# Weight parts of the first feed-forward interleaved by element, zones lengthened by 64 bytes

## The chip, the cores and the metric

The kernel runs on one core of one Trainium2 chip. The metric is the device time of one execution in microseconds (us); a lower time is better. An execution with a profile records what each engine did: TensorE (PE for matmuls, PEld for the weight loads in front of them), VectorE (DVE), ScalarE (ACT), GpSimd (POOL), and SyncE (SP), which only issues DMAs.

## What is computed

The reference, cut to what matters:

```python
B, H, S, D = 4, 8, 576, 64
# attention: 4 heads see the last 32 keys, 4 heads see every 32nd key
attn = softmax(where(mask, q @ k.T / 8, -1e9)) @ v
x = attn.transpose(0, 2, 1, 3).reshape(2304, 512)
x = ((x @ w_a) * (x @ w_b)) @ w_out                    # first feed-forward, 512 -> 1536 -> 512
y = (sigmoid(x @ w_gate) * (x @ w_val)) @ w_out2        # second feed-forward, same sizes
```

All of it is float32, and the result is held to float32 accuracy. TensorE's fast float32 form keeps fewer bits than float32, so the kernel splits each operand into a high and a low part and adds three products: high by high, low by high, high by low.

## The kernel before

**Memory.** Apart from some small tiles and one tile named `rest`, on-chip memory is cut into zones: twelve weight zones `w0` to `w11` of 12,288 bytes in each partition, four activation zones `x12` to `x15` of 8,192 bytes, and `h16` of 4,096 bytes. In the trace a zone appears as `w0p`, `x12p` and so on. `at(a, n, phase)` gives a view of a zone and makes the zone's tile on first use. In the built program all zones and all slices of them that TensorE reads with the fast float32 form start at distances from each other that are multiples of 512 bytes.

**First feed-forward.** The 2304 tokens are five tiles: four of 512 tokens (4 batches by 128 positions) and one of 256. For each tile the code goes through the 12 blocks `k` of the 1536 inner features. Each block has two products (line 923, from `x12` to `x15`) of 4 chunks by 3 terms, that is 24 matmuls, and, one block later, an output product (line 1013, from `h16`) of 12 matmuls. So a tile is 12 x 36 = 432 matmuls and the five tiles are 2160. Each matmul has its own weight load of 128 columns, which TensorE does while the matmul before it runs. The moving operand is 512 or 256 consecutive floats per partition.

**Its weights.** `convert` makes them during the first tile: 36 slices of 512 floats, three for each `k`. For each slice a DMA brings raw 64-bit words, ACT and DVE build a float32 from each (lines 482 and 491; it stands in every second float of a buffer), ACT writes its high part (line 499) and DVE its low part (line 503). Zone `wk` holds `w_a` high, `w_a` low, `w_b` high, `w_b` low, `w_out` high, `w_out` low, each 512 consecutive floats:

```python
def weight(m, k, h, phase=FIRST):
    return (k * 6 + m * 2 + h) * DM, DM, phase
```

While a tile is in the feed-forward, DVE also does the strided heads of the next tile's attention (lines 781 to 851), whose transposes (line 877) and splits (lines 890 and 894) TensorE and DVE do before that tile starts. PE does small attention matmuls (lines 563, 604 and 618) between its feed-forward matmuls.

**Second feed-forward.** It is done by Strassen's seven products on the same zones, reused in two later phases. All of its 2268 matmuls stand in line 1292, with 384 consecutive floats as moving operand and consecutive floats as weights.

**Order.** A planner at build time works out one list per engine, from estimated costs and due times. Each engine keeps its list; waits are by semaphores. At the start, PE is fed matmuls on a bfloat16 tile of zeros named `nil` (line 423) while it has nothing else to do; their weights are 128 consecutive bfloat16 values, their moving operand 512 columns.

Of the kernel before, what the change touches and what calls it, by code (L numbers as in the profile page):

```python
# [7 lines left out]
F32 = mybir.dt.float32  # L8
F32R = mybir.dt.float32r
# [13 lines left out]
P = 128  # L23
# [54 lines left out]
for _n, (_k, _w) in RINGS.items():  # L78
    if _n not in PLACE:
        PLACE[_n] = TOP  # L80
        TOP += _k * _w


def region_of(a):
    return next((r for r in REGIONS if r[0] <= a < r[0] + r[1]), None)
# [81 lines left out]
class Plan:  # L167
# [16 lines left out]
    def touch(self, op, reads=(), writes=()):  # L184

        for ranges, writing in ((reads, False), (writes, True)):
            for a, n, phase in ranges:
                b = a + n
                r = region_of(a)
                if r and self.phase.get(r, EARLY) != phase:  # L190

                    self.phase[r] = phase
                    c, d = r[0], r[0] + r[1]
                    self.seen = [(c, d, s[2], True) if s[0] < d and c < s[1] else s for s in self.seen]
                kept = []
                for s in self.seen:
                    c, d, other, wrote = s
                    if c < b and a < d and other is not op and (wrote or writing):
                        op.deps.append(other)
                        if writing and a <= c and d <= b:  # L200
                            continue
                    kept.append(s)
                self.seen = kept
                self.seen.append((a, b, op, writing))
        return op

    def add(self, eng, cost, fn, deps=(), key=0.0, take=(), free=(), size=0):
        op = Op()
        op.slack = self.slack
        op.eng, op.cost, op.fn, op.key, op.size = eng, cost, fn, key * 1e3, size  # L210
        op.deps = [d for d in deps if d is not None]
        op.take, op.free, op.slot, op.end = take, free, {}, None
        op.seq = len(self.ops)
        self.ops.append(op)
        for ring, owner in free:
            if ring in PLACE:
                taker, i = owner if isinstance(owner, tuple) else (owner, None)
                rings = [allowed for r, allowed in taker.take if r == ring]
                for allowed in rings if i is None else rings[i:i + 1]:
                    size = RINGS[ring][1]  # L220
                    for s in allowed:
                        a = PLACE[ring] + s * size
                        self.ends.append((a, a + size, op))
        return op
# [88 lines left out]
def dve(n):  # L313
    return (n + 66) / 0.96


def act(n):
    return (n + 105) / 1.2
# [22 lines left out]
def r32(ap):  # L341
    return ap.bitcast(F32)
# [3 lines left out]
def attention_moe_kernel(ctx, tc, qkv, sq, sk, sv, w1, w2, mask, ident, out):  # L346
    nc = tc.nc
    PE, ACT, DVE, POOL = nc.tensor, nc.scalar, nc.vector, nc.gpsimd
    engine = {"ACT": ACT, "DVE": DVE, "POOL": POOL}

    sb = ctx.enter_context(tc.tile_pool(name="sb", bufs=1))
# [10 lines left out]
    tiles = {}  # L362

    def at(a, n, phase=FIRST, dtype=F32):
        r = region_of(a)
        if r is None:
            v = rest[:, a - F0:a - F0 + n]
        else:
            if tiles.get(r, (None,))[0] != phase:
                name = f"{('w', 'x', 'h')[(r[0] >= X0) + (r[0] >= H0)]}{REGIONS.index(r)}"  # L370
                tiles[r] = phase, sb.tile([P, r[1]], F32, tag=name, name=f"{name}p{phase}")
            v = tiles[r][1][:, a - r[0]:a - r[0] + n]
        return v if dtype == F32 else v.bitcast(dtype)

    def xT(i, c):

        return at(X0 + (2 * i + c // 2) * XZONE, XZONE, FIRST, F32R).rearrange("p (c n) -> p c n", c=HK)
# [3 lines left out]
    add, touch = plan.add, plan.touch  # L381

    def buf(op, ring, shape, dtype=F32):
        s = op.slot[ring][0]
        if ring in PLACE:
            return at(PLACE[ring] + s * RINGS[ring][1], shape[1], FIRST, dtype)
        return sb.tile(shape, dtype, tag=f"{ring}{s}", name=f"{ring}{s}")
# [14 lines left out]
    for i, n in enumerate(TILES):  # L402
        begin.append(t)
        k = sum(g.i == i + 1 for g in GROUPS)
# [5 lines left out]
    def weight(m, k, h, phase=FIRST):  # L410

        return (k * 6 + m * 2 + h) * DM, DM, phase
# [37 lines left out]
    def raw(op, dtype=F32):  # L450
        return buf(op, "raw", [P, T * D], dtype)

    def convert(w, need, start=()):
        parts, done, merges = {}, {}, []
        tops = []

        def clear(op):
            for i in op.slot["c"]:
                tops.append(at(PLACE["c"] + i * DM, DM, FIRST, U32))
                POOL.memset(tops[-1], 0)  # L460

        c_top = add("POOL", 1000, clear, start, key=need(0, 0) - AHEAD - 10,
                    take=[("c", F_RING[:1]), ("c", F_RING[1:])])
        for c in range(3 * KF):
            k, m = divmod(c, 3)
            x = {}
            key = need(k, m) - AHEAD
            at_load = key - LEAD

            if k == 0 and m < 2:  # L470
                key -= EARLIER

            def load(op, x=x, k=k, m=m):

                x["raw"] = raw(op, U32)[:, :2 * DM]
                nc.sync.dma_start(
                    out=x["raw"].bitcast(U16)[:, :4 * DM - 1], in_=w[k, m].bitcast(U16)[:, 1:]
                )

            def top(op, x=x):  # L480
                x["t"] = tops[op.slot[f"t{id(w)}"][0]]
                ACT.activation(  # L482
                    out=x["t"].bitcast(F16).rearrange("p (n two) -> p n two", two=2)[:, :, 1],
                    in_=x["raw"].bitcast(BF16).rearrange("p (n four) -> p n four", four=4)[:, :, 2],
                    func=AF.Copy, scale=0.5,
                )

            def merge(op, x=x):
                u = x["raw"].rearrange("p (n two) -> p n two", two=2)[:, :, 0]
                x["f"] = u.bitcast(F32)  # L490
                DVE.scalar_tensor_tensor(  # L491
                    out=u, in0=u, scalar=13, in1=x["t"],
                    op0=ALU.logical_shift_right, op1=ALU.bitwise_or,
                )

            def high_part(op, x=x, k=k, m=m):
                hi, lo = (at(*weight(m, k, i), F32R) for i in range(2))
                parts[m, k] = hi, lo
                ACT.activation(out=hi, in_=x["f"], func=AF.Copy, scale=256.0)

            def low_part(op, x=x, k=k, m=m):
                hi, lo = parts[m, k]
                DVE.scalar_tensor_tensor(
                    out=lo, in0=x["f"], scalar=256.0, in1=r32(hi),
                    op0=ALU.mult, op1=ALU.subtract,
                )

            plan.slack = M2
            a = add("SP", 450, load, start, key=at_load, take=[("raw", (0, 1, 2))], size=1 << 19)
            b = add("ACT", act(512), top, [a, c_top], key, take=[(f"t{id(w)}", (0, 1))])  # L510
            end = c == 3 * KF - 1
            f = add("DVE", dve(512), merge, [b] + merges * end, key,
                    free=[(f"t{id(w)}", b)] + [("c", c_top)] * end)
            merges.append(f)
            g = touch(add("ACT", act(512), high_part, [f], key), (), [weight(m, k, 0)])
            h = touch(add("DVE", dve(512), low_part, [g], key, free=[("raw", a)]), (), [weight(m, k, 1)])
            done[m, k] = g, h
            plan.slack = 0
        return parts, done
# [481 lines left out]
    for n, g in enumerate(GROUPS):  # L1001
        if g.i == 0:
            attention(g, n * 1.5, OTHERS, True, [])
    W1, done1 = convert(w1, lambda k, m: begin[0] + span[0] * (k + m / 3) / KF)


# [20 lines left out]
    for i, n in enumerate(TILES):  # L1027
# [13 lines left out]
        o = (i % 2) * N2  # L1041
        acc = {}
        for k in range(KF):
            x = {}
            step = span[i] / KF
            key = begin[i] + k * step
# [397 lines left out]
    for j in NEED:  # L1444
        key = stage - 20 + 6 * NEED.index(j)
        s0 = 0
        while s0 < KS:
# [3 lines left out]
            o = (WO[j][s0][0], (s1 - s0) * 2 * WB2, THIRD)  # L1451
# [142 lines left out]
```

## Time and profile before

| | |
|---|---|
| runs, median (lowest to highest) | 903.76 us (903.71 to 905.16) |
| profiled execution | 903.51 us, of which the span of instructions is 901.7 us |
| granted TensorE clock, mean over the span | 1.000 |
| PE busy | 893.2 us (99%), 5170 matmuls |
| PEld busy | 802.6 us (89%), 5170 weight loads |
| DVE busy | 654.9 us (73%) |
| ACT busy | 405.7 us (45%) |

The span lies from the first to the last instruction; some 1.8 us of the execution lie outside it. [...]

### The profile page before, as it was taken

To read this page: it belongs to the slowest core of one execution; us is meant where nothing else is said; L and a number is where in the kernel's file an instruction comes from. 1 tells how busy PE (TensorE), PEld (TensorE's weight loads), DVE (VectorE), ACT (ScalarE), POOL (GpSimd) and SP (SyncE) were. 2 spreads that over 40 slices of the span, in tenths; PEclk is the share of its full clock that TensorE was granted. 3 is DMA by queue.
4 is the path that set the end of the run, shared out by engine and by line. 5 is a ranking of instruction groups with operands and counts; after the bars stand their busy time and mean duration, and the time that the engine had idled before them with its cause. 6 is when DMAs were issued, how large, how long until landed. Compare 5 with 4: busy or idle time off the path is not lost.

```text
span 901.7 us, 13664 instructions
## 1 busy us (share of the span) xinstructions
PE 893.2 (99%) x5170; PEld 802.6 (89%) x5170; DVE 654.9 (73%) x1078; ACT 405.7 (45%) x843; POOL 11.7 (1%) x23
## 2 busy tenths in 40 slices
PE   8999999999999999999999999999999999999998
PEld 4678888888888888888899999999999999999998
DVE  7999988998999878811328876675768458649491
ACT  5775644411242113311236655564666445435351
POOL 4000000000000000000000000000000000000000
PEclk9999999999999999999999999999999999999999
DMA  9666564312332124300035243645574588953501
GB/s 311 203 232 219 201 201 135 91 44 63 92 128 72 54 65 144 96 1 1 0 118 164 94 139 113 216 152 187 200 243 168 196 306 331 378 166 116 167 17 62
DMA packets 62513, 132.67 MB, mean 147 GB/s; under 512 B 5872, under 2 KB 37232, under 8 KB 61552
## 3 DMA queue, kind: packets, MB, share of 16 engines
q1 hardware_dynamic: 62160, 131.60, 43.9%
q8 instruction: 40, 0.66, 0.3%
q10 hardware_dynamic: 288, 0.21, 0.1%
q14 instruction: 25, 0.20, 0.1%
HBM read 97.19 MB, written 34.60 MB: 146 GB/s over the span
## 4 chain that ended last, share of the span: by engine, by line
PE 96%; DVE 3%; DMA 0%; ACT 0%; issue 0%; DVEq 0%
PE bank L1292 43%; PE bank L923 32%; PE bank L1013 16%; PE idle L423 1%; PE bank L563 1%; PE bank L618 1%; PE bank L604 1%; DMA rest<-w 0%; PE bank L877 0%; DVE rest L491 0%; PE bank L436 0%; DVE w8p L851 0%; DVE w9p L851 0%; DVE nm L575 0%; DVE x14p L630 0%
## 5 line engine op out<-in xcount | busy, mean ns | idle before, releaser
L947 ACT CAST h16p<-rest 128x512 fp32r<-128x512 f32 (+1 forms) x60 | 34.7, 579 | 144.1 <-PE bank L1013 140.1
L1304 DVE TENSOR_TENSOR rest<-bank,rest 128x384 f32<-128x384 f32 x84 | 46.4, 555 | 57.3 <-PE bank L1292 32.5
L943 DVE TENSOR_TENSOR rest<-bank,rest 128x512 f32<-128x512 f32 (+1 forms) x60 | 38.1, 635 | 54.4 <-PE bank L923 54.1
L1065 ACT COPY rest<-bank 128x512 f32<-128x512 f32 (+1 forms) x60 | 32.7, 545 | 93.1 <-PE bank L923 91.6
L1310 ACT COPY rest<-bank 128x384 f32<-128x384 f32 x84 | 40.1, 479 | 67.2 <-PE bank L1292 66.9
L951 DVE TENSOR_TENSOR h16p<-rest,h16p 128x512 fp32r<-128x512 f32 (+1 forms) x60 | 38.2, 636 | 29.1 <-PE bank L1013 23.6
L781 DVE TENSOR_TENSOR rest<-rest 128x320 f32<-128x320 f32 (+13 forms) x56 | 51.5, 920 | 1.3 <-DMA rest<-sq 0.5
L844 DVE TENSOR_TENSOR rest<-rest,s 128x320 f32<-128x320 f32 (+13 forms) x56 | 51.5, 920 | 0.9
L787 DVE TENSOR_REDUCE s<-rest 128x5 f32<-128x320 f32 (+13 forms) x56 | 51.2, 914 | 1.2
L851 DVE TENSOR_REDUCE rest<-rest 128x64 f32<-128x320 f32 (+13 forms) x56 | 51.2, 914 | 1.0
L482 ACT ACTIVATE rest<-rest 128x512 f16<-128x512 bf16 x36 | 28.4, 793 | 9.2 <-DMA rest<-w 9.1
L1202 DVE SCALAR_TENSOR_TENSOR rest<-rest 128x512 uint32<-128x512 uint32 x36 | 24.7, 688 | 10.2 <-ACT rest L1195 10.2
L1195 ACT ACTIVATE rest<-rest 128x512 f16<-128x512 bf16 x36 | 28.0, 790 | 5.9 <-DMA rest<-w 5.8
L1375 DVE TENSOR_TENSOR rest<-bank,rest 128x384 f32<-128x384 f32 x36 | 20.0, 557 | 11.8 <-PE bank L1292 11.0
L1314 ACT COPY bank<-bank 128x384 f32<-128x384 f32 x42 | 19.6, 467 | 18.6 <-PE bank L1292 18.2
L1369 ACT ACTIVATE rest<-bank 128x384 f32<-128x384 f32 x36 | 17.8, 493 | 21.4 <-PE bank L1292 21.2
L491 DVE SCALAR_TENSOR_TENSOR rest<-rest 128x512 uint32<-128x512 uint32 x36 | 24.5, 684 | 0.9 <-ACT rest L482 0.9
L581 ACT ACTIVATE rest<-bank,nm 128x96 f32<-128x96 f32 x56 | 18.3, 339 | 12.2 <-DVE nm L576 10.6
L1369 ACT ACTIVATE rest<-rest 128x768 f32<-128x768 f32 x18 | 15.2, 846 | 14.2 <-DVE rest L1304 13.8
L1292 PE MATMUL bank<-w8p,w10p 128*128 128x384 f32 x100 | 20.7, 334 | 0.0
L1375 DVE TENSOR_TENSOR rest<-rest 128x768 f32<-128x768 f32 x18 | 17.2, 953 | 0.7 <-ACT rest L1369 0.2
L1292 PEld LDWEIGHTS bank<-w8p,w10p 128*128 128x128 f32 x100 | 17.6, 188 | 0.0
(500 smaller groups left out, 2413.8 us busy)
## 6 DMA issues: line engine op xcount, KB each, us to landing
rest<-w SPq DMA_DIRECT2D x72, 511.8 KB, 4.2
h2d<-rest SPq DMA_DIRECT2D x18, 768.0 KB, 4.2
rest<-qkv SPq DMA_DIRECT2D x12, 416.0 KB, 4.2
w2p<-h2d SPq DMA_DIRECT2D x12, 384.0 KB, 5.5
w0p<-h2d SPq DMA_DIRECT2D x12, 384.0 KB, 5.5
w1p<-h2d SPq DMA_DIRECT2D x12, 384.0 KB, 5.5
out<-rest SPq DMA_DIRECT2D x24, 192.0 KB, 1.8
x2d<-rest SPq DMA_DIRECT2D x16, 256.0 KB, 2.1
```

The lines of the kernel that those rows point to most:

```text
L781: engine[op.eng].tensor_tensor(out=product(op, n), in0=x["k", h][:, :, :n, :], in1=x["q"][h // 2][:, e:e + nh, j:j + 1, :].to_broadcast([P ...
L787: DVE.tensor_reduce(out=weights_of(h, j, n), in_=x["p", op.deps[0]], op=ALU.add, axis=AX.X)
L844: engine[op.eng].tensor_tensor(out=product(op, n, "p (h d t) -> p h d t"), in0=x["v", h][:, :, :, :n], in1=weights_of(h, j, n).unsqueeze(2 ...
L851: DVE.tensor_reduce(out=xs[:, j, e:e + nh, :], in_=x["p", op.deps[0]], op=ALU.add, axis=AX.X)
L923: PE.matmul(x[tag][:, :n], ww[:, c * P:(c + 1) * P], xx(c), start=(u == 0 and c == chunks[0]), stop=(u == last and c == chunks[-1]),)
L943: DVE.tensor_tensor(out=x["g"], in0=x["b"][:, :n], in1=x["g"], op=ALU.mult)
L951: DVE.tensor_tensor(out=x["hl"], in0=x["g"], in1=r32(x["hh"]), op=ALU.subtract)
L1013: PE.matmul(ps[:, :n], ww[:, m * P:(m + 1) * P], x[xx], start=start, stop=stop)
L1292: PE.matmul(bank_of(where), at(*lhs(a, (0, 1, 0)[q], c), F32R), at(*rhs(b, (0, 0, 1)[q], c), F32R), start=p in OPENS and (q, c) == units[0 ...
L1304: DVE.tensor_tensor(out=at(*o), in0=bank_of("Z"), in1=at(*a), op=ALU.add)
L1310: "ACT", act2(NS), lambda op: ACT.copy(out=at(*o), in_=bank_of("Y")), [ops[after]], key - 20))
L1375: DVE.tensor_tensor(out=at(*o), in0=src(), in1=at(*o), op=ALU.mult)
```

## The change

The 512 high and 512 low floats of one weight slice, which lay one behind the other, now share the same 4,096 bytes alternately: high, low, high, low. A weight load of 128 columns then reads every second float over 1,024 bytes instead of 512 consecutive bytes. ACT writes the high part, and DVE reads it and writes the low part, with a step of two floats. For the planner, the writing of the high part now claims the space of both parts. Each zone's tile is 64 bytes longer, but for `x12`, `x13` and `x14`, so that zones made later move by a multiple of 64 bytes; what is read of them is unchanged. In the second feed-forward nothing but these addresses changes.

```diff
+LINE, SAME = 16, ("x12", "x13", "x14")
...
-                tiles[r] = phase, sb.tile([P, r[1]], F32, tag=name, name=f"{name}p{phase}")
+                tiles[r] = phase, sb.tile([P, r[1] + LINE * (name not in SAME)], F32, tag=name, name=f"{name}p{phase}")
...
             def high_part(op, x=x, k=k, m=m):
-                hi, lo = (at(*weight(m, k, i), F32R) for i in range(2))
-                parts[m, k] = hi, lo
+                o, n, phase = weight(m, k, 0)
+                v = at(o, 2 * n, phase, F32R).rearrange("p (n two) -> p n two", two=2)
+                parts[m, k] = hi, lo = v[:, :, 0], v[:, :, 1]
                 ACT.activation(out=hi, in_=x["f"], func=AF.Copy, scale=256.0)
...
-            g = touch(add("ACT", act(512), high_part, [f], key), (), [weight(m, k, 0)])
+            g = touch(add("ACT", act(512), high_part, [f], key), (), [weight(m, k, 0), weight(m, k, 1)])
```

The lists of all five engines in the built program are the same before and after, instruction by instruction, with the same engines waited for at the same places; only the access patterns and addresses differ. No instruction moves.

## Rows read from the trace of the kernel before

**Rows 1.** The page: busy time by engine, and the granted clock in slices.

```profile
span 901.7 us, 13664 instructions
PE 893.2 (99%) x5170; PEld 802.6 (89%) x5170; DVE 654.9 (73%) x1078; ACT 405.7 (45%) x843; POOL 11.7 (1%) x23
...
PEclk9999999999999999999999999999999999999999
```

**Rows 2.** Busy time of each engine in seven stretches (from:to us, then length).

```profile
0.00:30.00 30.00, 26.49 (x232) 14.36 (x233) 24.00 (x64) 18.55 (x65) 9.90 (x18) 1.00 0.85 275
30.00:128.00 98.00, 97.49 (x529) 79.43 (x528) 93.75 (x179) 66.09 (x126) 0.00 (x0) 1.00 0.65 208
128.00:232.00 104.00, 104.00 (x577) 85.13 (x576) 93.51 (x136) 30.14 (x80) 0.57 (x2) 1.00 0.32 97
232.00:338.00 106.00, 106.00 (x584) 86.83 (x583) 94.44 (x119) 27.96 (x74) 0.22 (x1) 1.00 0.27 83
338.00:448.00 110.00, 110.00 (x540) 89.53 (x539) 53.44 (x83) 27.69 (x68) 0.99 (x2) 1.00 0.15 50
448.00:502.00 54.00, 53.98 (x438) 53.25 (x437) 31.98 (x66) 26.72 (x56) 0.00 (x0) 1.00 0.36 118
502.00:902.00 400.00, 395.27 (x2280) 394.12 (x2278) 263.83 (x436) 208.53 (x376) 0.00 (x0) 1.00 0.53 183
```

**Rows 3.** The chain that ended last: start, length, line, matmuls in the piece.

```profile
5.78 3.67 PE idle L423 x17
...
303.27 5.44 PE bank L923 x24
...
462.54 2.88 PE bank L923 x24
...
552.12 346.28 PE bank L1292 x1996
```

**Rows 4.** The same chain from 128 to 140 us, around attention work on PE.

```profile
127.97 1.13 PE bank L923 x5
129.10 1.82 PE bank L1013 x8
130.92 0.44 PE bank L877 x4
131.35 0.94 PE bank L1013 x4
132.29 5.46 PE bank L923 x24
```

**Rows 5.** Matmuls of L923, then L1013, then L1292: PE busy, then PEld busy.

```profile
0.00:902.00 902.00, 315.16 (x1440) 248.96 (x1440) 1.00 0.44 147
0.00:902.00 902.00, 159.96 (x720) 125.42 (x720) 1.00 0.44 147
0.00:902.00 902.00, 394.04 (x2268) 393.08 (x2268) 1.00 0.44 147
```

**Rows 6.** Weight loads by line: count, busy us, mean ns of one.

```profile
L563 PEld LDWEIGHTS bank<-rest 128*64 128x64 f32 x224 | 7.9, 138 | 1.2 <-issue 1.2
L1013 PEld LDWEIGHTS bank<-h16p,w0p 128*128 128x128 f32 x12 | 1.5, 192 | 0.0
L1013 PEld LDWEIGHTS bank<-h16p,w7p 128*128 128x128 f32 x12 | 2.3, 188 | 0.5
```

**Rows 7.** Conversion on ACT and DVE: count, busy us, mean ns; then two single lines.

```profile
L482 ACT ACTIVATE rest<-rest 128x512 f16<-128x512 bf16 x36 | 28.4, 793 | 9.2 <-DMA rest<-w 9.1
L491 DVE SCALAR_TENSOR_TENSOR rest<-rest 128x512 uint32<-128x512 uint32 x36 | 24.5, 684 | 0.9 <-ACT rest L482 0.9
L951 DVE TENSOR_TENSOR h16p<-rest,h16p 128x512 fp32r<-128x512 f32 x11 | 7.6, 690 | 1.2 <-PE bank L1013 0.7 <-ACT h16p L947 0.2
...
L499 ACT ACTIVATE w11p<-rest x3: 648/657/672, 119.3 to 126.9; 128x512 fp32r<-128x512 f32 x3
...
L503 DVE SCALAR_TENSOR_TENSOR w11p<-rest,w11p x3: 682/684/685, 120.3 to 127.8; 128x512 fp32r<-128x512 f32 x3
```

**Rows 8.** Around the first transposes of the second tile: DVE, then weight loads.

```profile
129.75 0.68 DVE L851 TENSOR_REDUCE rest<-rest 128x64 f32<-128x512 f32 x1
...
130.53 0.58 PEld L877 LDWEIGHTS bank<-idt,rest 128*128 128x128 f32 x4
```

**Rows 9.** PE's waits for the conversion: us in total, times, longest us.

```profile
PE bank L923 <- ACT w2p L499: 0.4, 1, 0.4
...
PE bank L923 <- DVE w0p L503: 0.3, 1, 0.3
```

## The prediction, made before the changed kernel was run

> **What bounds the kernel now.** [...]
>
> The pace stands in the chain of waits, where a piece is a run of matmuls and its length holds no overlap [rows 3]. One matmul takes 5.44 / 24 = 226.7 ns for 512 columns, 346.28 / 1996 = 173.5 ns for 384, 2.88 / 24 = 120.0 ns for 256. From 256 to 512 columns it is 106.7 ns more, so a column costs 0.417 ns, and what is left in each of the three is 13.3 to 13.5 ns: a fixed extra that doesn't depend on the length. The bfloat16 matmuls at the start have the same 512 columns and take 3.67 / 17 = 215.9 ns, an extra of 2.5 ns [rows 3]. So each fast float32 matmul loses 10.8 ns against the bfloat16 form. The counts of the three lines are 1440, 720 and 2268 [rows 5]: 2160 x 10.8 = 23.3 us in the first feed-forward, 24.5 us in the second.
>
> Is this extra a constant of the form, or two streams in each other's way? Two rows speak for the second. It isn't always 13.3 ns: straight after the transposes of 131 us four matmuls take 0.94 / 4 = 235 ns each, and then the pace comes back to 227 [rows 4]; a pure constant would not wander. And it doesn't scale with the moving operand, only with there being one weight load for each matmul. TensorE's two read streams are the candidates: the moving operand goes through memory at 4 bytes each 0.417 ns, 9.6 bytes per ns. For the weights, a load of 64 columns takes 138 ns and one of 128 takes 188 to 192 [rows 6]; the difference for 64 columns is 50 to 54 ns, so 0.8 ns a column, or about 5 bytes per ns.
>
> **The change part by part.** *Interleaving.* A load of 128 columns now goes over 1,024 bytes in the same 100 to 107 ns (64 columns' difference, twice), which is 9.6 to 10.2 bytes per ns, the pace of the moving stream. Before, the moving stream gains about 512 bytes on the weights in each load, so it passes over every place they hold within such a distance. After, the two run side by side and keep the distance they start with. If what costs 10.8 ns is their meeting, it falls away wherever they start apart. I take the bfloat16 extra as the floor: 2160 x 10.8 = 23.3 us is the most that this can give. From below, nothing: 0 us if the extra belongs to the form. No row shows a float32 weight load with a step, so a loss is possible too (rivals). I take the upper end, since the wandering of [rows 4] is nearer to a meeting than to a constant.
>
> [...]
>
> *What DVE takes back.* In the first tile weights are made just ahead of their use, and the transposes before the second tile are loaded at 130.53 us, when DVE's last reduction for them ended at 129.75 + 0.68 = 130.43 us [rows 8]. PE can't reach that place sooner than DVE. DVE is busy for 93.75 of 98.0 us there [rows 2], so it can move up by at most 4.25 us, and only if all its own waits vanish. The first tile's share of the gain is 432 x 10.8 = 4.7 us; I let half of DVE's gaps close (2.1 us) and so lose 2.6 us. In the next tiles DVE has 10 and 12 us of gaps for a gain of 4.7 us each, so nothing is lost.
>
> *The steps of two on ACT and DVE.* DVE's line 491 writes with a step of two, line 503 without: 684 and 684 ns; line 951, all consecutive, takes 690 [rows 7]. So a step costs DVE nothing that a row shows. ACT's line 499 takes 657 ns with a step on its input alone; line 482, with steps on both sides, 793 [rows 7]. Bound: 0 to 136 ns x 36 = 4.9 us of ACT, which is busy 66 of 98 us there [rows 2]; hidden, but for the delay of one conversion, and PE's waits for them are 0.4 and 0.3 us in all [rows 9]. I take 0; if DVE's cover were gone each ACT step would be 0.1 us later, once for each block, 1.6 us at most.
>
> *Wider claim of the high part.* The lists and the places of waits stay, so 0.
>
> *Zones 64 bytes longer.* In the second feed-forward both streams stay consecutive, so the moving one still gains 512 bytes in each load, wherever it starts: I take 0. The bounds: down to the floor, -24.5 us; up to 235 ns as in [rows 4], 8.3 ns x 2268 = +18.8 us.
>
> Sum against the profiled execution's 903.5 us: -23.3 + 2.6 = -20.7, so 882.8 us; the median of the runs lies 0.25 us higher, so 883 us.
>
> **The rivals.**
>
> *The extra is the form's own.* Switching to float32 weights costs 10.8 ns however they lie in memory. For it: it is the same to 0.2 ns for 256, 384 and 512 columns [rows 3]. Against: 235 ns [rows 4]. Then 903 to 905 us.
>
> *The extra grows with the memory a load covers.* For it: the bfloat16 load covers 256 bytes and pays 2.5 ns, the float32 load 512 bytes and pays 13.3. A load over 1,024 bytes would pay at least 26.6, and the whole first feed-forward, 2160 x 13.3 = 28.7 us: slower, 932 us. It decides as soon as a matmul's extra rises above 13.3 ns. Against: nothing but the wandering. In the 256-column tile it has a harder form: if the load of every second float took twice its 107 ns, 214 ns, it would still hide behind 226.7 ns but not behind 120, and 432 x 94 = 41 us are lost, 945 us; the point is a load longer than the matmul.
>
> [...]
>
> *The shift spoils the second feed-forward.* If where the streams start matters at 64 bytes, its 2268 matmuls move by up to +18.8 us, which nearly eats the gain: 899 to 903 us with the forecast's gain, 915 to 922 without it. If it helps, 858 to 875 us.
>
> **How the numbers follow.** Forecast 0.57: 876 to 895 us on its own (half the gain to all of it and no loss to DVE, or some help in the second feed-forward). Both feed-forwards faster, under 876: 0.05. The form's own extra: 0.13. More memory, more extra, 905 to 933 us: 0.13; the harder form or worse, above 933: 0.05. The shift's loss 0.07, two parts in seven of which still end faster. Within 0.2% is about what a measurement of this kernel can tell from no change. Faster: 0.57 + 0.05 + 0.02 = 0.64; same 0.13; slower 0.23. The range from 876 to 932 leaves out the 0.05 below and some 0.08 above.
>
> **What would show it.** Right: in the chain, pieces of line 923 near 5.18 us for 24 matmuls and 2.62 us in the 256-column tile, line 1292 still at 173.5 ns, and DVE near full in the first tile with PE waiting at line 877 by about 131 us. If 5.44 stays, the extra was the form's. If it is 5.7 or more, the span of the load counts. If line 1292's pace moves, the 64 bytes do. If 5.18 shows but the end doesn't come forward, a wait of PE for DVE took it. Most likely to make me wrong: that a strided float32 load has a price no row shows, or that the gain differs from zone to zone.

## The result and the profile after

The changed kernel takes 915.24 us (median of 3 runs, 915.23 to 915.53) against 903.76 us: a ratio of 1.0123, with a 95% interval from 1.0100 to 1.0146. It became slower by 11.5 us, where 21 us less were forecast. All lines of the changed file from the zones on stand 3 or 4 further down: 923 is 927, 1013 is 1017, 1292 is 1296, 499 and 503 are 503 and 507.

The page of the changed kernel, against [rows 1]: the same number of instructions, the same full clock, and PE still 99% busy. PE took 10.4 us more, PEld 15.2 us more, DVE and ACT what they took before. PE's idle time grew by 1.4 us only (from 8.5 to 9.9): it is PE's own work that got longer.

```profile
span 913.5 us, 13664 instructions
PE 903.6 (99%) x5170; PEld 817.8 (90%) x5170; DVE 656.0 (72%) x1078; ACT 405.6 (44%) x843; POOL 11.5 (1%) x23
...
PEclk9999999999999999999999999999999999999999
```

The table by stretches of the changed kernel shows the same in two stages, against [rows 2]. From 30 to 128 us PE starts 520 matmuls where it started 529. From 128 to 232 us it has no idle time before or after, but starts 567 where it started 577.

```profile
30.00:128.00 98.00, 97.32 (x520) 80.57 (x521) 92.14 (x177) 65.73 (x127) 0.00 (x0) 1.00 0.64 208
128.00:232.00 104.00, 104.00 (x567) 86.51 (x566) 91.88 (x135) 30.05 (x80) 0.57 (x2) 1.00 0.31 97
```

The same table for the matmuls of one line over the whole span: lines 927, 1017 and 1296, against [rows 5]. PE is busy 4.8 us longer in the first, 2.9 us in the second and 3.3 us in the third. The third is the second feed-forward, of which nothing but addresses changed.

```profile
0.00:914.00 914.00, 320.00 (x1440) 256.85 (x1440) 1.00 0.44 145
...
0.00:914.00 914.00, 162.81 (x720) 129.54 (x720) 1.00 0.44 145
...
0.00:914.00 914.00, 397.37 (x2268) 396.40 (x2268) 1.00 0.44 145
```

The chain that ended last, in the changed kernel, against [rows 3] (start, length, line, matmuls in the piece):

```profile
83.86 5.59 PE bank L927 x24
...
100.60 5.53 PE bank L927 x24
...
314.45 2.76 PE bank L1017 x12
...
470.90 2.88 PE bank L927 x24
...
560.91 349.23 PE bank L1296 x1996
```

These lines show three paces. At 512 columns 24 matmuls take 5.53 or 5.59 us, 230.4 or 232.9 ns each, where they took 226.7; which value holds differs from block to block. At 256 columns the 2.88 us (120.0 ns) are what they were. At 384 columns 349.23 / 1996 = 175.0 ns stand against 173.5.

The durations of matmuls overlap (those of line 1292 last 334 ns each in the trace of before and start 173.5 ns apart), so a pace is read from the distances between starts. Nearly the whole difference adds up from these distances in the two traces (leaving out those with other work or a wait between the two): in the 512-column tiles their mean went from 227.5 to 231.8 ns, 4.3 ns x 1728 = 7.4 us; at 384 columns from 173.35 to 174.8, 1.46 ns x 2268 = 3.3 us; and the first matmul of the feed-forward came 0.7 us later (24.6 against 23.9 us). Together 11.4 us, against 11.8 between the two spans and 11.5 between the medians. Before that first matmul PE waited for DMAs, the longest of these waits not among PE's before. From the changed kernel's table of PE's waits (total, times, longest):

```profile
PE bank L567 <- DMA w7p<-qkv: 1.2, 1, 1.2
```

That the change makes these 0.7 us is not shown: in the experiments below the same matmul starts anywhere from 24.1 to 25.1 us, and at 25.0 in e3_zones_256, whose median is that of the kernel before.

The two conversion steps that write with a step of two, in the changed kernel (shortest/median/longest ns), against [rows 7]: 672 ns where ACT took 657, 685 where DVE took 684.

```profile
L503 ACT ACTIVATE w11p<-rest x3: 667/672/682, 121.6 to 129.3; 128x512 fp32r<-128x512 f32 x3
...
L507 DVE SCALAR_TENSOR_TENSOR w11p<-rest,w11p x3: 682/685/690, 122.5 to 130.2; 128x512 fp32r<-128x512 f32 x3
```

### The profile page after: what moved, and what is told of

It reads as the page before. It is cut to its first block, busy times and chain, and to the rows that moved or that the text cites. A ratio compares the mean times of both kernels' runs of the same rounds, so it can differ in the third digit from the quotient of the medians.

```text
span 913.5 us, 13664 instructions
## 1 busy us (share of the span) xinstructions
PE 903.6 (99%) x5170; PEld 817.8 (90%) x5170; DVE 656.0 (72%) x1078; ACT 405.6 (44%) x843; POOL 11.5 (1%) x23
## 4 chain that ended last, share of the span: by engine, by line
PE 94%; DVE 3%; DMA 2%; SPq 0%; ACT 0%; issue 0%; DVEq 0%
PE bank L1296 43%; PE bank L927 32%; PE bank L1017 16%; PE bank L622 1%; PE bank L567 1%; DMA w7p<-qkv 1%; DMA w5p<-qkv 1%; PE bank L608 1%; DMA rest<-w 0%; PE bank L881 0%; DVE rest L494 0%; DVE w8p L855 0%; DVE w9p L855 0%; DVE nm L579 0%; DVE x14p L634 0%
## 5 line engine op out<-in xcount | busy, mean ns | idle before, releaser
L1379 DVE TENSOR_TENSOR rest<-bank,rest 128x384 f32<-128x384 f32 x36 | 20.1, 557 | 12.5 <-PE bank L1296 11.8
L585 ACT ACTIVATE rest<-bank,nm 128x96 f32<-128x96 f32 x56 | 18.3, 340 | 11.9 <-DVE nm L580 10.4
L1373 ACT ACTIVATE rest<-rest 128x768 f32<-128x768 f32 x18 | 15.2, 845 | 14.4 <-DVE rest L1308 14.1
L1296 PE MATMUL bank<-x15p,w3p 128*128 128x384 f32 x88 | 17.6, 336 | 0.0
```

The source lines that it names most:

```text
L1296: PE.matmul(bank_of(where), at(*lhs(a, (0, 1, 0)[q], c), F32R), at(*rhs(b, (0, 0, 1)[q], c), F32R), start=p in OPENS and (q, c) == units[0 ...
```

## The experiments

The theory after the result: where the weights and the moving operand lie in memory sets the pace of a fast float32 matmul of 512 columns; the kernel before sat in the cheapest place for that length, and the change left it in two ways at once, by the step and by the 64 bytes. The rivals: one of the two parts alone does the harm, or a load with a step has a price of its own that grows with the memory it covers.

**Interleaving alone** (e1_step_only). The changed kernel with the zones' old lengths:

```diff
-LINE, SAME = 16, ("x12", "x13", "x14")
+LINE, SAME = 0, ("x12", "x13", "x14")
```

> High and low parts alternate by element, no zone is longer. Theory A (the step in the weight load costs, wherever the zones lie): matmuls of 512 columns go from 226.7 to some 233 ns as in those zones of the changed kernel that start in line with the moving operand, 1728 x 6 = 10 us, the 256-column tile stays at 120.0, the second feed-forward stays at 173.5 ns: 913 to 915 us. Theory B (the step is harmless and the uneven starts of the zones cost in both feed-forwards): 226.7 and 173.5 ns, 903 to 905 us.

Measured: 915.21 us, ratio 1.0119 (1.0100 to 1.0139) to the kernel before, just above the range of theory A. The chain of this kernel:

```profile
308.30 2.80 PE bank L1017 x12
311.10 5.60 PE bank L927 x24
...
470.19 2.88 PE bank L927 x24
...
564.11 346.26 PE bank L1296 x1996
```

Now most 512-column blocks take 233.3 ns a matmul (5.60 / 24), 256 columns are untouched, and the second feed-forward is back at 173.5 ns. The mean distance of starts rose by 6.2 ns, x 1728 = 10.7 us of the 11.2 us. So interleaving alone costs as much as the whole change, and the second feed-forward's loss is the work of the 64 bytes.

**The longer zones alone** (e2_zones_only). The changed kernel with the parts one behind the other again:

```diff
-                o, n, phase = weight(m, k, 0)
-                v = at(o, 2 * n, phase, F32R).rearrange("p (n two) -> p n two", two=2)
-                parts[m, k] = hi, lo = v[:, :, 0], v[:, :, 1]
+                hi, lo = (at(*weight(m, k, i), F32R) for i in range(2))
+                parts[m, k] = hi, lo
```

> Zones longer as in the change, weight parts consecutive as before. Theory A: the first feed-forward goes back to 226.7 ns or close, the second keeps the 175 ns that the changed kernel shows against 173.5 before (2268 x 1.6 = 3.6 us): 906 to 908 us. Theory B: the first feed-forward stays at 231 to 232 ns and the second at 175: 914 to 916 us.

Measured: 913.07 us, ratio 1.0095 (1.0078 to 1.0112), between the two ranges and in neither. Its chain:

```profile
300.21 5.49 PE bank L926 x24
305.70 2.77 PE bank L1016 x12
308.46 5.51 PE bank L926 x24
...
325.58 5.58 PE bank L926 x24
...
333.95 5.59 PE bank L926 x24
...
559.19 349.23 PE bank L1295 x1996
```

The 64 bytes alone spoil the 512-column blocks too: 228.8 to 232.9 ns a matmul in those shown, 231.2 in the mean (6.5 us), and they bring the 3.3 us of the second feed-forward. The 256-column tile became faster: 117.9 ns in place of 120.0, 0.9 us less. The costs of the two parts, 11.2 and 9.0 us, don't add: together they are 11.5 us. That both parts do harm fits the theory; that they don't add fitted no simple sum and asked for the pace itself.

The blocks shown are those of `w6`, `w7`, `w9` and `w10`. In the built program `x12` to `x15` all start at the same remainder by 256 bytes, and from these weight zones to them it is 0, 64, 128 and 192 bytes beyond a multiple of 256. Over all blocks of line 926 the mean pace at these four distances is 228.3, 229.9, 232.6 and 233.4 ns. The moving operands' own remainder is one and the same here, so it is their distance from the weights that counts.

**Paces by step and start** (m1_pace). A kernel that computes nothing of the reference: groups of 60 fast float32 matmuls on fixed operands in two zones of memory, each with its weight load, other engines idle. The other three kernels named pace are of the same kind.

```python
# weights' step in floats, start of the moving operand in floats, columns
for n in (512, 384, 256, 128):
    for step in (1, 2): CASES.append((step, 0, n))
for off in (4, 8, 16, 24, 32, 48, 64, 96, 128):
    for step in (1, 2): CASES.append((step, off, 512))
CASES += [(4, 0, 512), (0, 0, 512), (0, 0, 256), (0, 0, 128), (4, 0, 256), (2, 16, 256), (2, 32, 256), (2, 48, 256)]
```

> Computes nothing of the reference: 34 groups of 60 matmuls in the fast float32 form, each with its weight load, on data in place, three bfloat16 matmuls between groups. Columns 512, 384, 256, 128 with weights' step 1 and 2; then 512 columns with the moving operand starting 16 to 512 bytes further on; last a step of 4 and a step of 0 (one column repeated). If the extra of 13.3 ns comes from two streams meeting in memory, a step of 0 lowers it towards 2.5 ns, and the pace changes with the start. If the extra grows with the memory covered, a step of 4 costs more than 2, and 2 more than 1, for all starts. If it belongs to the form, steps of 0 and 1 pace alike. With 128 columns the weight load itself should be the limit: 107 to 120 ns if a load takes that long, and twice that at step 2 if a step halves the rate of loading.

Five groups of its chain: 512 columns with weights step 1, then step 2; the moving operand 64 bytes further with step 1; 256 bytes further; and 256 columns with step 4.

```profile
11.56 13.64 PE q0x L57 x60
25.20 14.00 PE q1x L57 x60
...
150.37 13.75 PE q0x L57 x60
...
267.37 13.64 PE q0x L57 x60
...
398.95 13.90 PE q0x L57 x60
```

Worked out from the distances of starts in each group's second half (ns a matmul, 512 columns; the start is that of the moving operand against the weights, in bytes; the 160 are from the two measurements of paces that follow, where the other starts up to 256 come out within 1 ns of these, save start 0 with step 2, which took 233.3 in the second and 235.6 in the third):

```
start            0      16     32     64     96     128    160    192    256    512
step 1         226.7  231.7  233.3  228.9  233.5  232.5  234.1  233.4  226.7  226.7
step 2         233.3  233.3  233.4  233.4  235.6  231.6  233.4  233.4  233.4  233.4
```

From start 0, a step of two changes nothing at 384 and 256 columns (173.35 and 120.0 ns). Two things follow. With consecutive weights only starts that are multiples of 256 bytes give 226.7 ns; the kernel before had all its zones there, and the kernel with longer zones alone has nearly these paces at its four distances. With a step of two no start does, and the start matters less (231.6 to 235.6). In the changed kernel's blocks of line 927 the distances 0, 64, 128 and 192 bytes take 232.9, 233.0, 231.3 and 230.7 ns: at the last two the step made the shifted zones cheaper, which is why the two costs don't add, though this table has 233.4 and not 230.7 for 192 bytes.

It also says that a load didn't get twice as long: with step 2 and 256 columns it still hides in 120.0 ns, and with 128 columns the pace is 117.8 ns against 111.7, while step 4 takes 233 ns under 256 columns (13.90 / 60 = 231.7 for the piece). So under 256 columns every second float costs nothing and every fourth 113 ns; why is not shown. It doesn't carry over to the moving operand, with which a matmul at every second float takes twice the time (451 ns for 512 columns against 226.9, in m2_pace).

Two of the signs named beforehand failed: weights of one repeated column take 231.6 ns under 512 columns, so a step of 0 neither lowers the extra nor paces like step 1 (at 256 and 128 columns it does pace like it); and a step of four takes 234.9 ns there, hardly more than a step of two.

**Zones 256 bytes longer** (e3_zones_256). The kernel before with the ends of four zones moved, so that all starts shift by multiples of 256 bytes:

```diff
+LINE, MORE = 64, ("w11", "w8", "x15", "w1")
...
-                tiles[r] = phase, sb.tile([P, r[1]], F32, tag=name, name=f"{name}p{phase}")
+                tiles[r] = phase, sb.tile([P, r[1] + LINE * (name in MORE)], F32, tag=name, name=f"{name}p{phase}")
```

> Weight parts consecutive; four zones (w11, w8, x15, w1) longer by 256 bytes instead of fourteen by 64, so that later zones move by multiples of 256 bytes. Theory (only the place of the two streams within 256 bytes matters): as before, 226.7 and 173.5 ns, 903 to 905 us. Rival (any move of the zones, or distances that are no multiple of 512, costs): in between, 906 to 913 us.

Measured: 904.27 us, ratio 0.9997 (0.9988 to 1.0007). Its chain has the old paces, 226.7 and 173.5 ns:

```profile
306.03 5.44 PE bank L926 x24
...
554.88 346.28 PE bank L1295 x1996
```

So longer zones are harmless as such; the remainder by 256 bytes is what counted.

**The step in the output product alone** (e4_step_out_only). Only the weights `w_out` (m = 2) are interleaved, zones as before:

```diff
+                parts[m, k] = hi, lo = (v[:, :, 0], v[:, :, 1]) if m == 2 else [
+                    at(*weight(m, k, i), F32R) for i in range(2)]
```

> No zone is longer; only the weights of the output product (a third of the loads) alternate by element, the other two thirds are consecutive as before. Theory (each stepped load of a 512-column matmul costs some 6.5 ns): 576 of 1728 matmuls, 3.8 us, 907 to 908.5 us, line 1013's pieces of 12 at 2.80 us and line 923's of 24 at 5.44. Rival (the step upsets the pace of its neighbours too, or the cost sits in the writing of the parts): 910 us or more, or 903.8.

Measured: 907.77 us, ratio 1.0042 (1.0028 to 1.0056). First a piece of the kernel before, then the chain of this one:

```profile
300.55 2.72 PE bank L1013 x12
...
302.95 2.80 PE bank L1018 x12
305.75 5.45 PE bank L928 x24
...
555.95 346.26 PE bank L1297 x1996
```

Line 1018 goes from 2.72 to 2.80 us for 12 matmuls, 6.7 ns each, and line 928 stays. 6.7 ns x 144 output matmuls in each of four tiles = 3.9 us, against 3.5 us measured. The price is paid matmul by matmul, by those whose weights have the step.

**What the extra consists of** (m2_pace). As before, 59 groups of 48 (six more than announced), now with fewer weight columns, with one column of weights repeated 128 times or one of the moving operand 512 times, with other lengths, and with bfloat16:

```python
# type, weight columns, weights' step, moving operand's step and start, columns (a step of 0 repeats one column)
CASES = [("r", n, 1, 1, 0, 512) for n in (128, 96, 64, 32)]
CASES += [("r", 128, 1, 0, 0, 512), ("r", 128, 0, 0, 0, 512), ("r", 128, 0, 1, 0, 512), ("r", 128, 2, 0, 0, 512)]
...
```

> Computes nothing of the reference: 53 groups of 48 matmuls with their weight loads, four bfloat16 matmuls between groups. Varied: columns of weights (128, 96, 64, 32), one repeated column for weights or moving operand, steps of 1 to 4, moving columns from 508 to 128, the bfloat16 form, and the moving operand's start in steps of 32 bytes. If the extra over the column time is the two streams meeting, it goes when the moving operand is one repeated column (pace near 216 ns at 512), and shrinks with fewer weight columns. If it is the form's own, it stays at 13.3 ns in all of these. If the pace locks to some raster, 508, 504 and 496 columns show the same time as 512 or jump. Starts 256 bytes apart should pace alike, those between worse at 512 columns (229 to 235 ns).

Its chain: loads of 128 and of 32 columns; the moving operand one repeated column; the weights one repeated column; weights with step 2 under one repeated moving column; and the moving operand with a step of two:

```profile
9.71 10.89 PE q0x L66 x48
...
45.33 11.12 PE q1x L66 x48
...
57.33 10.49 PE q0x L66 x48
...
80.08 10.99 PE q0x L66 x48
...
91.94 10.49 PE q1x L66 x48
...
139.80 21.65 PE q1x L66 x48
```

Divided by 48: 226.9, 231.7, 218.5, 229.0, 218.5 and 451 ns. A load of a quarter of the columns makes the matmul slower, and weights that all come from one place, which no stream can pass over, don't help. Only a moving operand that stays in one place does, and then the weights' step is nothing. The bfloat16 groups of 512 columns settle at 215.8 ns, with consecutive weights or a step of two. So some 8 of the 10.8 ns, from 226.9 to 218.5, are there only while the moving float32 operand is swept; the other 3, from 215.8 to 218.5, stay with the float32 form even when it stands still.

The start also counts at other lengths here. 384 columns take 173.3 ns at most starts, but 176.7 at 96 and 175.6 at 128 bytes. That is part of the second feed-forward's loss: sorted by distance (0, 64, 128, 192 bytes), its matmuls with the longer zones alone take 174.8, 173.6, 175.9 and 174.9 ns, and why 0 and 192 bytes cost there what they don't cost here stays open. 256 columns take 120.0 at start 0 and 113.35 at 192 bytes; with a step of two (m1_pace) 192 bytes takes 120.0, so there the step has a price at this length too.

**The last tile at 192 bytes** (e5_last_tile_192). The kernel before, with the columns of the 256-token tile 48 floats further in its zones:

```diff
-            return xT(i, 0)[:, :, (g.i % 2) * N2 + g.b * g.n:][:, :, :g.n]
+            return xT(i, 0)[:, :, (g.i % 2) * N2 + late(g.i) + g.b * g.n:][:, :, :g.n]
...
-            x["hh"] = buf(op, "hh", [P, N2], F32R)[:, :n]
+            x["hh"] = buf(op, "hh", [P, N2], F32R)[:, SHIFT * (n < N2):][:, :n]
```

> The kernel before, unchanged but for the tile of 256 tokens: its columns in the x zones and in h16 start 192 bytes further on (the slots are for 512 tokens, so there is room). Theory (the pace hangs on where the moving operand starts against the weights): 432 matmuls at 113.4 instead of 120.0 ns, as in the group of the second table with 256 columns and this start, 2.9 us less: 901 to 901.8 us. Rival (in the kernel the loads go through slices 512 bytes apart and the pace of single groups doesn't carry over): 903.5 to 905 us.

Measured: 903.18 us, ratio 0.9991 (0.9981 to 1.0001). Its chain in that tile:

```profile
461.61 1.41 PE bank L1020 x12
463.02 2.83 PE bank L930 x24
```

The time lies between the two ranges. The pace fell to 117.9 ns (2.83 / 24), a third of the way to 113.35. That would be 2.1 ns x 432 = 0.9 us, which is what the medians differ by, but the interval reaches past 1: a gain is not certain. Why it isn't all of the way stays open. It isn't the many slices, for eight slices in turn still take 113.3 ns in m3_pace; and with longer zones alone (e2_zones_only) the blocks of `w3` and `w10`, at this distance, did take 113.0 to 115.5 ns by pair of zones, those of `w0` and `w8` 117.0 to 118.5.

**More lengths and repeats** (m3_pace). 38 groups: lengths from 416 to 504, starts with step 2, and moving operands that repeat 128, 32, 8 or 4 floats:

```python
# weight columns, weights' step, moving operand's period (0: none) and start, columns (step 9: eight slices in turn)
...
CASES += [(128, s, 0, 0, n) for n in (416, 432, 464, 480, 496, 504) for s in (1, 2)]
...
CASES += [(128, s, p, 0, 512) for p in (128, 32, 8, 4) for s in (1, 2)]
...
```

> Computes nothing of the reference: groups of 48 matmuls as in the second table. Varied: weight columns 128, 64, 32 at steps 1 and 2; 416 to 504 columns at both steps; starts of the moving operand at step 2; a moving operand that repeats 128, 32, 8 or 4 consecutive floats; 256 columns with loads that go through eight slices. Theory (the extra is the moving operand's own reading of fresh memory, and the load only shifts its rhythm): repeating 128 or 32 floats keeps 226 to 233 ns, and only periods so short that a piece of memory is used again at once come near 218.7; fewer weight columns at step 2 pace like 128; no start at step 2 gets below 226.7. Rival (each stepped load has its price for the columns it loads): 64 and 32 columns at step 2 come back to the pace of step 1, and all of 416 to 504 columns pay some 6 ns more at step 2 than at 1.

Its chain: 432 columns with step 1 and 2, and 512 columns that repeat 32 floats, then 8 floats, with step 1:

```profile
101.36 9.40 PE q0x L64 x48
...
111.64 9.29 PE q1x L64 x48
...
285.51 11.36 PE q0x L64 x48
...
310.13 10.46 PE q0x L64 x48
```

At 432 columns (and at 416: 186.7 ns against 188.3) the step is cheaper, at 480 and 504 it makes no difference (216.7 and 226.65), at 464, 496 and 512 it costs 2 to 9 ns. A price that each load with a step pays can't do that. The other sign of that rival did come: with 64 and 32 weight columns the step costs 1.1 and 1.7 ns (231.1 against 230.0, 233.3 against 231.7), not the 7 to 9 of 128 columns, so how much is loaded has a part in it. The repeats, with consecutive weights: 4 or 8 floats 218.7 and 217.75 ns, 128 floats 226.65, and 32 floats 236.7, above the range given. With 256 columns and consecutive weights a start of 192 bytes takes 113.3 ns, also with loads that go through eight slices in turn, and 16 bytes to either side 119.3 and 119.2.

**Nearly no load at all** (m4_pace). 18 groups were announced and 20 stand in the kernel; loads of 128, 16, 4 and 1 columns under a swept moving operand, and repeats of 8, 16, 64 and 256 floats:

```python
CASES = [(c, 1, 0, 0, 512) for c in (128, 16, 4, 1)]
CASES += [(c, 1, 0, 16, 512) for c in (16, 4, 1)]
CASES += [(c, 1, 0, 0, 256) for c in (128, 16, 1)]
CASES += [(c, 1, 8, 0, 512) for c in (16, 1)]
CASES += [(128, s, p, 0, 512) for p in (8, 16, 64, 256) for s in (1, 2)]
```

> This kernel computes nothing of the reference: it measures paces, 18 groups of 48 fast float32 matmuls as in the measurements before, other engines idle. The open point: is the extra of the swept moving operand there when there is nearly no weight load beside it, or do loads and moving operand have to read at the same time? Loads of 128, 16, 4 and 1 columns are tried under 512 swept columns (starts 0 and 64 bytes) and under 256; then moving operands that repeat 8, 16, 64 and 256 floats. Theory one, the moving operand's own reading: with a load of one column the pace at 512 columns stays between 226 and 236 ns from either start, and the pace rises between a repeat of 8 floats (217.75) and of 32 (236.7) whatever the weights' step. Theory two, two reads at the same time: the pace falls with the load, to 219 ns or less at one column, from 231.7 at 32 columns.

Its chain: one weight column under 512 swept columns from start 0 and from 64 bytes, and under 256; one weight column under 8 repeated floats; and 16 repeated floats with 128 weight columns:

```profile
45.33 10.99 PE q1x L63 x48
...
81.15 11.10 PE q0x L63 x48
...
106.09 5.45 PE q1x L63 x48
...
123.76 10.51 PE q1x L63 x48
...
157.83 11.62 PE q0x L63 x48
```

With a load of a single column the swept 512 columns still take 229 to 231 ns (10.99 and 11.10 over 48), more than the 226.7 beside a full load in m1_pace. Eight repeated floats take 219. So the extra is there with nearly no weights to meet, and the rival that two reads have to coincide falls. Repeats of 64 and 256 floats pace as the sweep does, 226.65 ns with consecutive weights and 235.5 with a step of two, so reading the same 256 bytes again and again costs as much as reading on; 16 floats take 242 and 244. Loads do have a hand in it at 256 columns: 120.0 ns beside a load of 128 columns, 113.35 beside one of 16 or of 1.

## Why the prediction was wrong

**What bounds the kernel**: the forecast takes all of its gain from the pace of PE's own matmuls, and nothing else turned out to count. PE is idle for 0.5 us from 30 to 128 us and not at all from there to 448 us [rows 2]; in the changed kernel it is 0.7 us of the first stretch and none from 128 to 232 us. The order didn't move, and of PE's waits for DVE one of 0.2 us is new.

**The step that failed** is "If what costs 10.8 ns is their meeting, it falls away wherever they start apart." It isn't the meeting of two streams. A load from one repeated column leaves 229 ns, a load of one column 229 to 231, and a quarter of a load 231.7; only a moving operand that stays within 8 floats comes down to 218, with either step. Of the 10.8 ns against bfloat16, 8 to 9 go when the moving float32 operand stands still or repeats 8 floats (218.5 and 217.75 ns), and 2 to 3 stay even then. Nor is bfloat16's 2.5 ns, taken as the floor, reached by any fast float32 group of 512 columns. What weights do by their step and distance comes on top, and from where the kernel before stood it only added at 512 columns (from 226.7 to between 228.9 and 235.6 ns in the table of m1_pace). The wandering of [rows 4] was read as a sign of a meeting; it shows that the extra isn't constant, and no more. In m1_pace the first group, on fixed operands, does the same after its bfloat16 matmuls: gaps of 228 to 236 ns for half a dozen matmuls, then 226.7. Rows of before alone couldn't tell the two apart, and the three numbers (13.3 to 13.5 ns for 256, 384 and 512 columns) that looked like a constant were those of one start, a multiple of 256 bytes everywhere.

**The forecast gain of 23.3 us** became a loss of 7.4 us in the changed kernel, and of 10.7 us where the zones kept their lengths (e1_step_only), all of it in the 512-column tiles. With the step in place the shift gave back 3.3 us there, as much as it cost in the second feed-forward; that the whole change costs nearly what the step alone does is by chance.

**Zones 64 bytes longer, taken as 0**, was mis-sized: 3.3 us in the second feed-forward, within the bounds given. The reasoning behind the 0, that a stream gaining on another passes everything wherever it starts, fell with the meeting. Without the step the shift cost 5.7 us in the first feed-forward as well (9.0 less 3.3).

**The rivals.** "The shift spoils the second feed-forward" had the mechanism, at a sixth of its bound. "The extra grows with the memory a load covers" had the sign at 512 columns, at half its price (6.7 ns from start 0 in m1_pace, not 13.3), but not as a rule: from start 0, 256, 384 and 504 columns pay nothing for the step (120.0, 173.35 and 226.65 ns with either) and 416 and 432 gain by it (1.6 ns at 416). Its harder form, a load of twice the length, didn't happen (120.0 ns at 256 columns). That 915.24 us lies in the ranges of both (915 to 922 and 905 to 933) is luck: neither had a loss in each feed-forward. Of the signs, "If line 1292's pace moves, the 64 bytes do" held; line 923's pieces came to 5.53 or 5.59 us in the blocks shown, between 5.44 and 5.7, for which no reading was given. "The form's own extra" was right that the extra doesn't leave with the meeting, and wrong that it has one size.

**Steps on ACT and DVE** at 0 were right: 15 ns on ACT and 1 on DVE in the slices shown, 6 and 3 in the mean of all 36, and the two waits of PE for them in [rows 9] are 0.3 us each after the change. **What DVE takes back**, 2.6 us, was never put to the test, since no gain came.

**What the weight load has to do with it** is the smaller part: the extra is there beside loads of one column (229 to 231 ns in m4_pace), but the load's step and place move a matmul of 512 columns between 226.7 and 235.6 ns (m1_pace), and its number of columns moves one of 256 between 113.35 and 120.0 (m4_pace).

**What stays open** is why the pace settles where it does: why 504 and 512 columns take the same 226.65 ns, why 256 bytes is the period, why 16 repeated floats take 242 ns and 8 take 218, and why the same operands (step of two, start 0) take 233.3 ns in two measurements and 235.5 in the third. No run resolves single accesses to memory, and no simple sum over starts gives the 231.8 ns of the changed kernel exactly.

## What to carry to other kernels

The fast float32 matmul of 512 columns had an extra over bfloat16 that was there for the most part only while its moving operand was swept (226.9 ns, 218.5 with one repeated column, 215.8 in bfloat16; m2_pace), and the place of the operands against each other (here the remainder by 256 bytes) and the weights' step moved it by up to 9 ns in 227 (m1_pace): for 512 columns, keep zones that TensorE reads together at multiples of 256 bytes (226.7 ns with consecutive weights, 228.9 to 234.1 at the other starts tried), and look at the pace again after any edit that shifts addresses. A small extra that is the same for several shapes may be the floor of the best place and not a cost that can be removed. Before costing an edit on "two streams collide", measure the pace with one of them standing still.

## What the runs showed of the hardware that was not expected

- The distance of two operands sets the pace of a whole stage: zones longer by 64 bytes cost 9.0 us of 904 (e2_zones_only), by 256 bytes nothing (e3_zones_256, ratio 0.9997).
- A moving operand of every second float32 takes 451 ns for 512 columns, twice the 226.9 of consecutive ones (m2_pace); weights of every second float change a matmul by -2.5 to +9 ns (m1_pace, m3_pace).
- At 512 columns from start 0, fewer weight columns make the matmul slower: 226.7 ns at 128, 230.0 at 96 and 64, 231.7 at 32 columns (m2_pace). At 256 columns they make it faster: 120.0 at 128, 113.35 at 16 (m4_pace).
- At 128 and at 192 columns a matmul with 128 weight columns takes the same 111.7 ns (m2_pace), so there its length doesn't set the pace; the weights do move it, to 117.8 at 128 columns with every second float (m1_pace).
- The lengths are not even steps: 496, 504, 508 and 512 columns take 223.4, 226.65, 227.4 and 226.65 ns (m2_pace).
